# Thirty loads of 16-byte rows in SP's queue of a decode layer: one set before the ninth V, one before the last piece of the down weights

## The chip, the cores and the metric

The kernel runs on one core of one Trainium2 chip. The metric is the device time in microseconds (us); lower is better. Times of several runs are given as a median with the lowest and the highest.

## The reference, cut to what matters

One token of each of B = 4 sequences goes through attention over a cache and then through a gated MLP:

```python
q = (layernorm(x) @ wq)                       # 4 x 32 heads x 128
scores = einsum("bhqd,bhkd->bhqk", q, k_cache) * 128 ** -0.5   # 8192 keys
o = einsum("bhqk,bhkd->bhqd", softmax(scores), v_cache)
h = x + o @ wo                                # D = 512
g, u = layernorm(h) @ w_gate, layernorm(h) @ w_up              # F = 1792
out = h + (sigmoid(g) * u) @ w_down
```

The K cache and the V cache hold 4 x 32 x 8192 x 128 bf16 values each, 268.4 MB each. The weights together are 13.9 MB. All of it is read once.

## The kernel before, in words

The 128 pairs of sequence and head are worked off in NU = 32 units of four heads. A unit needs one K load and one V load of 8192 KB each; every load fills one of three slots of the buffer `KV` (128 partitions x 64 KB a slot). The list `order` gives the order of the loads: k0, k1, v0, k2, v1, ..., k31, v30, v31; entry n goes into slot n mod 3, so entry 18 is the ninth V (v8), which follows k9.

All large transfers are issued by SP, in this order (L466 to L500):

- `wq` (one load, L466), then the 63 whole K and V loads (L482). Entry n waits until entry n - 3 has been used up: a K until the DVE step `maxima` has passed the memset of `dummy` (L324), a V until the last matmul group of its weighted sum (L358). The last V, v31, is loaded in two halves `vh0`, `vh1` (L479).
- `wo` in three pieces of 2048, 1536 and 512 KB (L488), `wg` (L490) and `wu` in two pieces (L494), all of which wait for the last K to be used up.
- `wd` (the down weights) in three pieces `wd0`, `wd1`, `wd2` of 1024, 512 and 256 KB (`WDT`, L498), after v30 has been used up.
- half of the output (`out0`, L500); ACT issues `out1`. Then SP waits for both and ends (L502, L504).

Every DMA has a semaphore that counts 16 when it has landed (in `prog.dma`). SP works its list in order: what stands behind a waiting instruction waits too. Unit by unit, DVE transposes K in 16 chunks (`k_chunk`, L309), PE multiplies them with the query (L318), DVE finds the maxima (L324 to L331), ACT takes the exponential (L332), and PE forms the weighted sum of the V of the unit before (`pv`, L358, L374). At the end PE projects with `wo`, a layer norm follows, then gate and up (L432), and PE multiplies with `wd` in 14 steps (`down`, L457): steps 0 to 7 wait for `wd0`, 8 to 11 for `wd1`, 12 and 13 for `wd2`. DVE adds the residual (L463), and the two halves of the output go out.

Of the kernel before, what the change touches and what calls it, by code (L numbers as in the profile page):

```python
# [6 lines left out]
BF16 = mybir.dt.bfloat16  # L7
# [6 lines left out]
class _Prog:  # L14
# [51 lines left out]
    def emit(self, eng, fn, waits=(), incs=1, ch=None):  # L66
        todo = self._waits(eng, waits)
        key = ch or eng
        tok = self.token(key, incs) if incs else None
        self._put(eng, todo, key, fn, incs, 1)  # L70
        return tok
# [34 lines left out]
def bass_sequential_preLN__mha_block_cached__glu_gated_glu__decode_kernel(  # L106
# [13 lines left out]
    _, H, S, DH = A_k_cache.shape  # L120
# [15 lines left out]
    WDT = (0, 8, 12, 14)  # L136
# [3 lines left out]
    prog = _Prog({"p2d": "dve", "d2d": "dve", "a2d": "dve", "d2p": "pe", "a2p": "pe",  # L140
                  **{f"k{i}": "dve" for i in range(NSL)}, **{f"v{i}": "pe" for i in range(NSL)}})
    emit = prog.emit

    with ExitStack() as es:
        def SB(name, shape, dt):
            return es.enter_context(nc.sbuf_tensor(name, shape, dt))
# [19 lines left out]
        rs = SB("rs", [128, 1], FP32)  # L166
        ident = SB("ident", [128, 16], BF16)
        dummy = SB("dumm", [128, 2], FP32)

        kTb = kT[:, :].bitcast(BF16)  # L170
        KVw = KV[:, :].bitcast(FP32)
# [11 lines left out]
        def reg(slot, off, size):  # L183
            return KV[:, slot * SLOT + off:slot * SLOT + off + size]
# [20 lines left out]
        for k in keys:  # L205
# [12 lines left out]
        t_x = prog.dma("act", "x", lambda e: e.dma_start(x_bf, A_x.rearrange("b s d -> (b s) d")))  # L218

        t0 = emit("pool", lambda e: e.memset(ident[:, :], 0.0))  # L220
        t_ident = emit("pool", lambda e: e.affine_select(
            out=ident[:, :], in_=ident[:, :], compare_op=ALU.not_equal, fill=1.0, base=0,
            pattern=[[-1, 16]], channel_multiplier=1), [t0])
# [24 lines left out]
        def layernorm(src, waits, dst):  # L248
            a = emit("dve", lambda e: e.bn_stats(bst, src), waits)
            a = emit("dve", lambda e: e.bn_aggr(agg, bst), [a])  # L250
            a = emit("dve", lambda e: e.tensor_scalar(std[:, 0:1], agg[:, 1:2], EPS, None, op0=ALU.add), [a])
            a = emit("act", lambda e: e.activation(std[:, 1:2], std[:, 0:1], ACT.Sqrt), [a])
            a = emit("dve", lambda e: e.reciprocal(std[:, 0:1], std[:, 1:2]), [a])
            t_row = emit("dve", lambda e: e.tensor_scalar(
                row, src, agg[:, 0:1], std[:, 0:1], op0=ALU.subtract, op1=ALU.mult), [a])

            def f(e):
                ins = None
                for c in range(NC):
                    ins = e.matmul(cols(bank[XS], c), row[:, c:c + NC * 127 + 1:NC], ident[0:B, 0:B],  # L260
                                   start=(c == 0), stop=(c == NC - 1), skip_group_check=True)
                return ins
            a = emit("pe", f, [t_row, t_ident])
            return t_row, emit("dve", lambda e: e.tensor_copy(dst, bank[XS][:, 0:NC * B]), [a])
# [4 lines left out]
        _, t_xn = layernorm(x_bf, [t_x], xnT)  # L269
# [191 lines left out]
        for t in range(NFT):  # L461
# [4 lines left out]
        prog.dma("sp", "wq", lambda e: e.dma_start(reg(2, 0, NC * H * DH), A_wq.rearrange("(p c) f -> p (c f)", p=128)),  # L466
                 tok=t_wq)
        for n, (x, u) in enumerate(order):
            w = t_qp if n == 2 else None
            if n >= 3:  # L470
                y, o = order[n - 3]
                w = t_pv[o] if y == "v" else t_kd[o]
            slot = slots[x, u]
            halves = (x, u) == order[-1]
            cache = A_v_cache if x == "v" else A_k_cache
            src = cache[u % B, HU * (u // B):HU * (u // B + 1), :, :].rearrange("h (p r) d -> (h p) (r d)", p=32)
            if halves:
                for i in range(2):
                    prog.dma("sp", f"vh{i}", lambda e, src=src, slot=slot, i=i: e.dma_start(  # L479
                        reg(slot, i * SLOT // 2, SLOT // 2), src[:, i * SLOT // 2:(i + 1) * SLOT // 2]), [w], tok=t_vh[i])  # L480
                continue
            prog.dma("sp", f"{x}{slot}", lambda e, src=src, slot=slot: e.dma_start(reg(slot, 0, SLOT), src), [w],  # L482
                     tok=toks[x, u])
# [11 lines left out]
                reg(1, 16384 + (NC + 2 * i) * F, 2 * F), wu_src[:, 2 * i * F:2 * (i + 1) * F]), [k_done], tok=t_wu[i])  # L495
        wd_src = B_w_down.rearrange("(p t) f -> p t f", p=128)
        for i in range(len(WDT) - 1):
            prog.dma("sp", f"wd{i}", lambda e, i=i: e.dma_start(  # L498
                wd_v[:, WDT[i]:WDT[i + 1], :], wd_src[:, WDT[i]:WDT[i + 1], :]), [v_done], tok=t_wd[i])
        t_out = [prog.dma(("sp", "act")[x], f"out{x}", lambda e, x=x: e.dma_start(  # L500
            out.rearrange("b s d -> (b s) d")[:, HD * x:HD * (x + 1)], o_sb[32 * x:32 * x + B, :]), [t_o]) for x in range(2)]
        emit("sp", lambda e: e.nop(), t_out, incs=0)  # L502

        with nc.Block() as block:  # L504
            @block.sync
# [46 lines left out]
```

## Time and profile before

| | |
|---|---|
| time, median of 3 runs | 1283.34 us (1282.71 to 1283.39) |
| the profiled execution: time, span | 1282.72 us, 1281.0 us |
| bytes moved, mean rate over the span | 550.93 MB, 430 GB/s |
| PE, DVE, ACT busy | 784.0, 818.6, 51.1 us |
| SP's waits for DVE (L324) before a load | 1030.6 us in 31 waits |
| issue of k9, issue of v8 (SP) | 312.62 us, 346.90 us |
| issue of `wd0`, `wd1`, `wd2` (SP) | 1253.54, 1254.01, 1257.14 us |
| issue of the output (SP) | 1278.93 us |

Positions are us from the start of the span. A DMA issue on SP shows as an instruction of the queue (SPq); the transfer that it starts is seen in the DMA rows and in its time to landing. A transfer is cut into packets; the trace records the start, length and size of each packet, and the moment of each increment of a DMA's semaphore.

### The profile page before, as it was taken

To read this page: it belongs to the slowest core of one execution; us is meant where nothing else is said; L and a number is where in the kernel's file an instruction comes from. 1 tells how busy PE (TensorE), PEld (TensorE's weight loads), DVE (VectorE), ACT (ScalarE), POOL (GpSimd) and SP (SyncE) were. 2 spreads that over 40 slices of the span, in tenths; PEclk is the share of its full clock that TensorE was granted. 3 is DMA by queue.
4 is the path that set the end of the run, shared out by engine and by line. 5 is a ranking of instruction groups with operands and counts; after the bars stand their busy time and mean duration, and the time that the engine had idled before them with its cause. 6 is when DMAs were issued, how large, how long until landed. Compare 5 with 4: busy or idle time off the path is not lost. (4 is left out here: it accounts for less than half of the span.)

```text
span 1281.0 us, 13420 instructions
## 1 busy us (share of the span) xinstructions
PE 784.0 (61%) x5253; PEld 271.1 (21%) x5253; DVE 818.6 (64%) x1120; ACT 51.1 (4%) x106; POOL 4.3 (0%) x18
## 2 busy tenths in 40 slices
PE   1577665557755557655557655567555567555576
PEld 0122212122212222212222212222122222122222
DVE  2777776566665567665566765666766576756671
ACT  0000000000000000000000000000000000000001
POOL 1000000000000000000000000000000000000000
PEclk9998888789888799878898887898788898878897
DMA  9999999999999999999999999999999999999998
GB/s 426 424 425 430 449 426 426 434 445 430 426 436 440 434 426 436 438 436 426 432 436 442 426 428 434 446 428 426 436 444 430 426 436 440 434 426 436 436 424 330
DMA packets 11475, 550.93 MB, mean 430 GB/s; under 512 B 1212, under 2 KB 1224, under 8 KB 2760
## 3 DMA queue, kind: packets, MB, share of 16 engines
q1 hardware_dynamic: 11448, 550.77, 99.5%
q8 instruction: 7, 0.11, 0.0%
q14 instruction: 4, 0.03, 0.0%
q10 hardware_dynamic: 16, 0.01, 0.0%
HBM read 550.77 MB, written 0.00 MB: 430 GB/s over the span
## 5 line engine op out<-in xcount | busy, mean ns | idle before, releaser
L318 PE MATMUL PS<-kT,Lq 128*128 128x512 bf16 x2048 | 584.1, 416 | 442.7 <-PEq L51 428.6
L309 DVE STREAM_TRANSPOSE kT<-KV 128x1024 f32<-128x1024 f32 x512 | 617.5, 1233 | 199.5 <-DVEq L51 192.8
L318 PEld LDWEIGHTS PS<-kT,Lq 128*128 128x128 bf16 x2048 | 178.8, 103 | 849.3 <-issue 747.4
L358 PE MATMUL PS<-KV,PTz 128*16 128x512 bf16 x2048 | 120.5, 388 | 6.8 <-PEq L51 4.0
L381 DVE STREAM_TRANSPOSE kT<-PS 128x128 f32<-128x128 f32 x32 | 10.1, 317 | 144.6 <-DVEq L51 144.6
L338 DVE STREAM_TRANSPOSE PTz<-E_sb 32x512 bf16<-32x512 bf16 x128 | 89.9, 703 | 3.7 <-DVEq L51 0.7
L374 PE MATMUL PS<-kT,selc 128*1 128x128 f32 x1024 | 64.4, 403 | 28.2 <-PEq L51 27.9
L358 PEld LDWEIGHTS PS<-KV,PTz 128*16 128x16 bf16 x2048 | 58.7, 111 | 66.4 <-issue 20.7
L332 ACT ACTIVATE E_sb<-PS,negm 128x512 bf16<-128x512 f32 x32 | 22.0, 688 | 1171.6 <-DVE negm L331 1171.6
L325 DVE TENSOR_REDUCE mxp<-PS 128x1 f32<-128x512 f32 x32 | 22.1, 691 | 41.8 <-DVEq L51 41.8
L374 PEld LDWEIGHTS PS<-kT,selc 128*1 128x1 f32 x1024 | 27.6, 97 | 64.0 <-issue 43.6
L367 ACT ACTIVATE kT<-PS 128x512 f32<-128x512 f32 x32 | 19.1, 598 | 37.3 <-PE PS L358 37.3
L382 DVE TENSOR_SCALAR OT<-kT,rs 128x4 f32 (+1 forms) x32 | 7.3, 229 | 7.4 <-DVEq L51 7.2
L331 DVE STREAM_TRANSPOSE negm<-mxb 128x32 f32<-128x32 f32 x32 | 6.8, 212 | 4.7
L346 DVE STREAM_TRANSPOSE mxt<-mxb 128x32 f32<-128x32 f32 x32 | 6.8, 212 | 4.7
L302 DVE TENSOR_TENSOR Lq<-q_all,mask 128x32 bf16<-128x32 bf16 x32 | 9.8, 305 | 0.0
L327 DVE STREAM_TRANSPOSE mxt<-mxp 128x32 f32<-128x32 f32 x32 | 6.8, 212 | 4.7
L329 DVE TENSOR_SCALAR mxb<-mxr 128x32 f32<-128x32 f32 x32 | 5.8, 182 | 5.2 <-DVEq L51 0.6
L328 DVE TENSOR_REDUCE mxr<-mxt 128x1 f32<-128x32 f32 x32 | 6.0, 187 | 4.7
L344 DVE COPY mxb<-mxr 128x32 f32<-128x32 f32 x32 | 5.8, 181 | 4.7
L343 DVE TENSOR_REDUCE mxr<-mxt 128x1 f32<-128x16 f32 x32 | 5.4, 170 | 4.7
L347 DVE RECIPROCAL rs<-mxt 128x1 f32<-128x1 f32 x32 | 5.2, 164 | 4.7
(53 smaller groups left out, 60.9 us busy)
## 6 DMA issues: line engine op xcount, KB each, us to landing
KV<-in_A_v_cache_dram SPq DMA_DIRECT2D x2, 4096.0 KB, 46.2
KV<-in_A_wq_dram SPq DMA_DIRECT2D x1, 4096.0 KB, 12.2
KV<-in_A_wo_dram SPq DMA_DIRECT2D x1, 2048.0 KB, 23.1
KV<-in_B_w_gate_dram SPq DMA_DIRECT2D x1, 1792.0 KB, 29.4
KV<-in_B_w_up_dram SPq DMA_DIRECT2D x2, 896.0 KB, 22.0
KV<-in_A_wo_dram SPq DMA_DIRECT2D x1, 1536.0 KB, 26.5
KV<-in_B_w_down_dram SPq DMA_DIRECT2D x1, 1024.0 KB, 22.4
KV<-in_A_k_cache_dram SPq DMA_DIRECT2D x32, 50.5
```

What stands on the lines that cost most here:

```text
L302: t_lq[u] = emit("dve", lambda e, i: e.tensor_tensor(dst, bass.AP(raw(q_all), i * (4 * T3) + 4 * (u - T3 * t), [[NU * 4, 128], [1, 4], [0, ...
L309: t_tr[u, c] = emit("dve", lambda e: e.transpose(kT[:, (c % 2) * TW:(c % 2 + 1) * TW], KVw[:, o:o + TW]), w, ch="d2p")
L318: ins = e.matmul(bank[SBK], Lq[:, t, 31 - c:31 - c + 128], rhs, start=(c == 0 and t == 0), stop=(c == NT - 1 and t == 3))
L325: a = emit("dve", lambda e: e.tensor_reduce(mxp[:, 0:1], bank[SBK], AX.X, ALU.max), [t_sc[u, NT - 1], t_pool], ch="d2d")
L327: a = emit("dve", lambda e: e.transpose(mxt[:, :], mxp[:, :]), [a], ch="d2d")
L332: t_exp[u] = emit("act", lambda e: e.activation(E_sb[:, :], bank[SBK], ACT.Exp, bias=negm[:, 0:1], scale=SCALE, accum_out=sgp[:, 0:1]), [t ...
L338: return [e.transpose(PTz[32 * q:32 * (q + 1), :].rearrange("p (r q c) -> p r q c", r=4, q=4)[:, :, q, :], E_sb[32 * q:32 * (q + 1), :].re ...
L358: made.append(e.matmul(PS[32 * j:32 * j + 16, ob:ob + 512], lhsT, KV[:, slot * SLOT + 512 * k:slot * SLOT + 512 * (k + 1)], start=(k < 4), ...
L367: t_ocp[u] = emit("act", lambda e: e.activation(O_sb, bank[OBK], ACT.Copy), [t_pv[u]], ch="a2p")
L374: made.append(e.matmul(PS[32 * h:32 * h + 1, 512 * EX:512 * EX + 128], selc[:, 4 * h + q:4 * h + q + 1], rhs, start=(q == 0), stop=(q == 3 ...
L381: a = emit("dve", lambda e: e.transpose(OTf[:, :], bank[EX][:, 0:128]), [t_ex[u]], ch="d2d")
L382: t_ot[u] = emit("dve", lambda e, i: e.tensor_scalar(bass.AP(raw(OT), i * (4 * T3) + 4 * (u - T3 * t), [[NU * 4, 128], [1, 4]]), OTf[:, 0: ...
```

## The change

A tile `probe` (128 x 128 bf16) and thirty semaphores are added. `probes(n)` issues fifteen loads on SP: load m takes 8 values (16 bytes) from each of the first m rows of `wq` in HBM to the first m partitions of `probe`. One set is issued in front of entry 18 of the order (v8), the other in front of the last piece of the down weights (`wd2`). None of the thirty loads waits for anything, and nobody reads `probe`; SP's last instruction waits for all thirty semaphores besides the two of the output.

```diff
+        probe = SB("probe", [128, 128], BF16)
...
+        t_probe = {(n, m): None for n in range(2) for m in range(1, 16)}
+        for key in t_probe:
+            prog.sems["pr%d_%d" % key] = es.enter_context(nc.semaphore("s_pr%d_%d" % key))
+
+        def probes(n):
+            for m in range(1, 16):
+                t_probe[n, m] = prog.dma("sp", f"pr{n}_{m}", lambda e, m=m: e.dma_start(
+                    probe[0:m, 8 * m:8 * m + 8], A_wq[0:m, 0:8]))
...
         for n, (x, u) in enumerate(order):
+            if n == 18:
+                probes(0)
             w = t_qp if n == 2 else None
...
         for i in range(len(WDT) - 1):
+            if i == len(WDT) - 2:
+                probes(1)
             prog.dma("sp", f"wd{i}", lambda e, i=i: e.dma_start(
...
-        emit("sp", lambda e: e.nop(), t_out, incs=0)
+        emit("sp", lambda e: e.nop(), [*t_out, *t_probe.values()], incs=0)
```

In the compiled program SP has fifteen more waiting instructions at its end. They wait for the thirty probe semaphores, two at a time, and stand before the waits for the output, the last of them together with that for `out1`. The instructions of PE, DVE, ACT and GpSimd are the same, in the same order.

## The prediction

> **What bounds the kernel now.** I read the page's slices first, then its DMA queues, SP's waits, the chain that ended last, and SP's instructions at the end in order of time.
>
> ```profile
> PE   1577665557755557655557655567555567555576
> ...
> DMA  9999999999999999999999999999999999999998
> ...
> q1 hardware_dynamic: 11448, 550.77, 99.5%
> ```
>
> All 16 DMA engines work from the first slice to the last while PE is busy 5 to 7 tenths: the kernel lasts as long as its slowest DMA engine has packets, plus a short end. SP's waits show how much room its list has:
>
> ```profile
> SPq L482 <- DVE dumm L324: 1030.6, 31, 37.2
> SPq L482 <- PE PS L358: 130.1, 29, 4.5
> ```
>
> SP idles for most of the run, and a K load lands 50.5 us after its issue (page, DMA issues) though its bytes need 19.35 us (distance of two landings): more than one whole load is always queued behind the running one. At the end this turns:
>
> ```profile
> 1253.54 0.42 SPq L498
> 1253.96 0.05 issue
> 1254.01 23.15 DMA KV<-in_B_w_down_dram
> 1277.15 0.04 issue
> 1277.20 1.27 PE PS L457 x12
> ```
>
> The last steps wait for pieces of the down weights. The semaphore records say whose fault it is: fifteen increments of `wd2` arrive from 1274.65 to 1276.33, the sixteenth at 1277.79. One DMA engine runs 1.46 us behind the next and 3.14 us behind the first, and `wd1` shows the same (1275.73, then 1277.16). Delay on this engine moves the end one for one; delay on another is first taken up by 1.5 to 3.1 us of slack.
>
> **SP's time, first set.** It is issued when k9's issue has ended (312.95) and before v8's wait, which ends at 346.90, 33.9 us later. SP's issues cost 0.33 us on the 63 whole loads (0.57 at worst); the 4-row store takes 0.35. Fifteen at 0.35 are 5.3 us, at 0.57 8.6 us, both inside the wait: nothing. If the wait were gone, v8 would be issued 5.3 us later, and its 36.1 us to landing still cover that.
>
> **SP's time, second set.** Here SP is held back: the issue of `wg` takes 8.76 us, `wd1` 3.09, `wd2` 1.24. Counting packets issued less packets finished at the ends of the held issues (`wo2`, `wg`, `wd1`, `wd2`) gives 79, 80, 78 and 79 per engine: SP gets on when some packets have been finished. A set puts at most 30 packets on one engine (15 data, 15 increments). From 1257.1 the engines work on 4 KB packets of `wo` at 0.16 us, so 30 of them are 4.8 us; SP's own 15 x 0.35 = 5.3 us runs beside that. `wd2`, issued until 1258.38 now, would be issued until about 1263.7. Its first packet starts at 1273.43, and the first load of the run shows 1.0 us from issue (0.80) to first packet (1.83): 8.7 us to spare, cost nothing. `out0` stands behind it on SP and waits until 1278.93 anyway.
>
> **The DMA engines' time.** This is on the path. The 4-row store of `out0` shows how few rows are spread: its semaphore jumps at 1279.40, at the end of the issue, and then rises four times; its records hold four data packets and four increments. So m rows give m pairs of a 16-byte packet and an increment on m engines. The price of a pair: 4-byte increments take 9 ns and let the next packet start 6 ns later; at the other end the two output halves, whose 512-byte pairs follow each other on the same engines, start 29 to 45 ns apart. Packets of 2048 bytes cost 80 ns and of 4096 bytes 156 ns back to back, so a fixed part of 4 ns and the bytes. A pair of 16 bytes is therefore between 15 and 45 ns; I take 30, the middle, since the 16 bytes are nearer to the 4 and the engine must still fetch. An engine that is in every load carries 30 pairs: 0.9 us (0.45 to 1.35). Spread evenly, 240 pairs over 16 engines are 15 each: 0.45 us (0.23 to 0.68). The end moves by what falls on the slowest engine, and I do not know its place: if it is in all loads, +0.9; if in none, 0, since 1.35 us on any other engine stays below 1.46 us of slack. I take +0.45. The Trainium skill ("DMA: Bandwidth & Descriptors", "Why a DMA increments its semaphore by 16 and not by 1") says that such a DMA uses the lowest-numbered engines, as many as the rows; the four packets and the jump of the semaphore agree, which engines they are no view shows. By it one engine carries all 30 pairs, and the sum would be 0.9 or 0.
>
> **The waits at the end.** SP's issue of `out0` ends at 1279.29 and its wait for `out1` at 1280.20: 0.91 us idle. Fifteen waiting instructions at 17 ns each, with 0.04 us of issue between (chain), are 0.86 us and fit. At 0.1 us each they would be 1.5 us, 0.6 too long, but the wait for `out0` ends 0.41 us later still, so at most 0.2. I take 0. None can be held: the second set lies in the rings ahead of `wd2`, which has landed before.
>
> **Sum.** The profiled execution took 1282.72 us, its span and 1.72 around it; 0 + 0 + 0.45 + 0 makes 1283.2. It lies 0.62 below the median of 1283.34, so the forecast is 1283.8. About 0.2% (2.6 us) is what a measurement of this kernel can tell from no change; 0.45 is inside.
>
> **Rival 1, small writes that hold up their engine (slower).** The price above is that of sending. The records of landing say more: on the four engines of the output the second half's increments land 0.17 us after the first half's (1280.06 and 1280.24, 1280.18 and 1280.36), though they were sent 30 to 50 ns apart. Something takes 0.17 us per small DMA at the far end. If it holds the engine's stream back, 30 loads take 5.1 us on the engine that has them all; on the slowest engine this adds 5.1, on the first one 5.1 - 3.1 = 2.0 us, in the middle 3.5: 1286.8. The point from which it decides is 0.09 to 0.19 us a load: 2.6 us over 30 loads without slack, 5.7 with all of it. Against it: a large load's increment also waits for its data, and 8 packets of 2418 ns and one increment repeat every 19.35 us, so one increment costs 6 ns; fifteen in a row no row shows.
>
> The same with a longer price: each 16-byte write waits out a full trip. The shortest from an increment's packet to its landing is 0.30 us (load of `x`), so 30 are 9 us, less up to 3.1 of slack: 5.9 to 9.0, 1289 to 1292. The Trainium skill ("DMA: Bandwidth & Descriptors", "Specifications") states that writes under 512 bytes are done as read-modify-write; that speaks for this price if each trip is waited for. No data packet of under 512 bytes is in this trace's loads, so it stands neither confirmed nor refuted.
>
> **Rival 2, a queue of few places (slower).** If SP is held by the number of transfers in flight, not of packets, `wd2` comes late. At its issue eight are in flight now (`wo1` to `wd2`); with the probes 23. Were eight the limit, the eighth probe would wait for `wd1` (1277.16), and eight issues of 0.35 us take `wd2` to 1280.0; with 1.0 to its first packet, 0.64 for eight packets and 0.45 to land it is there at 1282.1 instead of 1277.79: +4.3, 1287.6. It decides as soon as a probe's issue takes over 1 us on average, 15.8 us from 1257.1 to 1272.9. For it: the issues here are slow; against it: `wd0` took 0.42 us with seven in flight.
>
> **Rival 3, the lag goes elsewhere (faster).** The slowest engine's lag grows in this trace from 2.50 to 3.48 us while a 16 KB instruction fetch runs (1242 us). SP's longer program can move a fetch to another engine. At best the end comes 1.46 us earlier: 1281.9, still within 0.2%; a larger gain needs the lag of seven engines to go, for which nothing speaks.
>
> **That the loads cost nothing at all** gives 1283.3 and belongs to the forecast.
>
> **Chances.** Forecast (no change within 0.2%, rival 3 in its likely size included): 0.56. Rival 1 at 0.17 us a load 0.21, at a full trip 0.10, rival 2 0.07: slower 0.38. Faster by over 0.2%: 0.06. The forecast alone spans 1281.9 to 1284.9 (1.46 less, or 1.35 and the waits' 0.2 more). The range takes in the first rival whole (1285.3 to 1288.5) and the second; its low end is cut to 1282.3. Left out are most of the full trip and half of the gains.
>
> **What the profile after would show.** In the packet records: 240 data packets of 16 bytes, 120 around 360 us (k9 lands about 363) and 120 between `wd1` and `wd2`. Right if SP's probe issues take about 0.35 us before the wait of L494 (formerly L482), `wd2` is issued by 1266, and the lag of the last engine at `wd2` stays between 1.5 and 4 us. Rival 1: one engine's packets behind the first set start 2.6 us or more late, and the lag at each later landing has grown by that. Rival 2: probe issues of over 1 us, and `wd2` landing as one late group of all engines. Wrong altogether if the rate before 1230 us is under 430 GB/s on all engines, or the final waits run past 1 us.

## The result and the profile after

The changed kernel takes 1285.69 us (18 runs, 1285.43 to 1285.96); the kernel before takes 1283.34 us in the same comparison. The ratio is 1.0019, with a 95% interval of 1.0012 to 1.0026: 2.35 us slower. That is inside the predicted range and, at 0.18%, just inside the 0.2% that the forecast allowed for no change, but five times the 0.45 us that its sum had. The profiled execution took 1285.75 us, its span is 1284.0 us.

The page's slices and its DMA queues, to be set beside those of before:

```profile
DMA  9999999999999999999999999999999999999997
...
q1 hardware_dynamic: 11928, 550.78, 99.4%
```

The 480 new packets are 240 of 16 bytes and 240 increments; the 16 engines still work from end to end. SP's waits:

```profile
SPq L494 <- DVE dumm L334: 1026.9, 31, 37.1
SPq L494 <- PE PS L368: 130.0, 29, 4.5
...
SPq L516 <- DMA out_dram<-KV: 0.2, 1, 0.2
```

SP's issues cost nothing: its waits for L334 before the loads are 3.7 us shorter in all (1030.6 before), less than the 5.28 us that the first set's issues take out of one of them. The last wait is shorter too (0.2 us, was 0.9), because fifteen added waits stand ahead of it. SP's instructions in order of time around the first set:

```profile
312.88 0.33 SPq L494 DMA_DIRECT2D KV<-in_A_k_cache_dram  x1
313.25 5.28 SPq L228 DMA_DIRECT2D probe<-in_A_wq_dram  x15
346.48 0.36 SPq L494 DMA_DIRECT2D KV<-in_A_v_cache_dram  x1
```

Its fifteen issues end 27.9 us before v8's. The rate while these packets pass is another matter. Two stretches, in each line the busy times and then granted clock, DMA share and GB/s, first before, then after:

```profile
340.00:360.00 20.00, 12.07 (x122) 4.60 (x120) 12.59 (x24) 1.38 (x3) 0.00 (x0) 0.98 1.00 433
360.00:365.00 5.00, 0.26 (x1) 0.14 (x2) 1.65 (x2) 0.00 (x0) 0.00 (x0) 0.50 1.00 433
```

```profile
340.00:360.00 20.00, 11.75 (x120) 4.57 (x120) 12.21 (x24) 1.37 (x3) 0.00 (x0) 0.94 1.01 433
360.00:365.00 5.00, 0.00 (x0) 0.00 (x1) 1.36 (x2) 0.00 (x0) 0.00 (x0) 0.50 0.97 354
```

For 5 us the DMA engines move 354 GB/s instead of 433: (433 - 354) x 5 us is 0.4 MB, 0.9 us of the whole rate. Packets of 64 KB make the rate of so short a stretch coarse, but the landings agree. Against two loads' distance (2 x 19.35 us) after v7's, v8's sixteen increments come 1.0 us late in the mean, the first 0.64 and the last 1.70 us, and the last engine keeps this to the end. Few bytes were added; the engines were held up, though the share counts them as busy.

The end of the chain that ended last:

```profile
1264.10 17.11 DMA KV<-in_B_w_down_dram
1281.20 0.04 issue
1281.25 0.43 PE PS L467 x4
```

Now the chain runs through `wd2`, and only the last four matmuls follow it; before, it ran through `wd1`, and twelve followed. The last piece lands 2.41 us after the piece ahead of it (1278.80 to 1281.20), before 0.63 us: +1.77 us. Not all of that counts. PE's instructions in order of time, after:

```profile
1277.69 1.75 PE L467 MATMUL PS<-KV 128*4 128x256 bf16 x24 [1.67 <-DMA KV<-in_B_w_down_dram]
1281.25 0.38 PE L467 MATMUL PS<-KV 128*4 128x256 bf16 x4 [1.80 <-DMA KV<-in_B_w_down_dram]
```

PE waits 1.80 us for the last piece. The granted clock was 1.00 in this stretch of this execution, so PE was through early with the first 24 matmuls. At a clock of 0.50 all 28 take 3.15 us when the last piece comes in time (e3, below); from the landing of the first piece, at 1277.56, they would end at about 1280.8 instead of 1281.7. Against such an execution about 0.8 us of the 1.77 remain.

### The profile page after: what moved, and what is told of

It is laid out like the page before. It is cut to its first block, busy times and chain, and to the rows that moved or that the text cites. A ratio compares the mean times of both kernels' runs of the same rounds, so it can differ in the third digit from the quotient of the medians.

```text
span 1284.0 us, 13465 instructions
## 1 busy us (share of the span) xinstructions
PE 785.2 (61%) x5253; PEld 271.3 (21%) x5253; DVE 818.2 (64%) x1120; ACT 51.0 (4%) x106; POOL 4.2 (0%) x18
## 5 line engine op out<-in xcount | busy, mean ns | idle before, releaser
L384 PE MATMUL PS<-kT,selc 128*1 128x128 f32 x1024 | 64.4, 403 | 28.1 <-PEq L51 27.9
```

The lines of the kernel that those rows point to most:

```text
L384: made.append(e.matmul(PS[32 * h:32 * h + 1, 512 * EX:512 * EX + 128], selc[:, 4 * h + q:4 * h + q + 1], rhs, start=(q == 0), stop=(q == 3 ...
```

## The experiments

Theory: each of the small loads costs an engine not its sending (12 ns) but the time of its increment, and the engine that lands last has 12 of the 15 loads of each set, those of 4 rows and more. In the trace after, on that engine, the increments of the second set land at 1278.98, 1279.16, 1279.35 and so on to 1281.02, every 0.17 to 0.20 us, and that of the last piece follows at 1281.20. Its 16-byte packets had been sent from 1278.31 to 1278.44, every 12 ns; then two packets of the last piece went, and the third took 0.90 us instead of 0.08. (The records name no engine; a packet is put to the engine whose packet before ends where it starts.) So the 1.77 us have three parts: 0.14 us of sending, 0.81 us of the one held packet, and 0.82 us because the last piece's own increment lands 1.29 us after it was sent, 0.46 before. Rivals: the 16-byte writes hold the engine; the 16-byte reads from HBM do; all engines meet at the same rows or partitions; SP's longer program.

Two measures stand beside each time. Step A is how much later v8's last increment lands than two loads' distance after v7's (0.00 us before). Step B is the distance from the last increment of `wd1` to that of `wd2` (0.63 us before). The median of the kernel before is 1283.2 to 1283.3 us in each comparison, and one comparison's ratio is known to about 0.09%.

**Each set alone.**

```diff
 # e1: without the second set
-            if i == len(WDT) - 2:
-                probes(1)
 # e2: without the first set
-            if n == 18:
-                probes(0)
```

> Only the first set (before v8). Theory (each small load's increment holds its DMA engine for 0.12 to 0.18 us, and the slowest engine, which has 12 of the 15 loads, moves the end): the lag that this engine gets at v8 in the trace after, 1.4 us, stays to the end: +0.9 to +1.4 us on the kernel before. Rival (the first set costs only its sending, and the rest of the loss is the end's): under +0.4 us. Rival (SP's longer program moves an instruction fetch, and that is the loss): about half of it, +1.2, with no step at v8.

> Only the second set (before the last piece of the down weights). Theory: the last increment of that piece lands 1.77 us later than by its distance from the piece before, and the end moves by +1.3 to +1.8 us; together with the first set alone about the +2.35 us of the whole change. Rival (the first set is all of it): under +0.4 us.

The first set alone: 1284.67 us, ratio 1.0011 (1.0002 to 1.0020), +1.40 us; step A 1.79, step B 0.64. The second alone: 1283.97 us, ratio 1.0006 (0.9997 to 1.0015), +0.70 us; its 11 runs (1283.88 to 1284.26) lie above all runs of before (up to 1283.59). Step A 0.02, step B 2.40. So 1.40 + 0.70 = 2.10 of the 2.35 us, and each set costs where its packets pass. The second was expected at 1.3 or more: its increment came as late as expected, the end did not. PE's instructions in order of time in e2, then in e3 (below), where the last piece is in time:

```profile
1275.82 2.72 PE L467 MATMUL PS<-KV 128*4 128x256 bf16 x24 [1.67 <-DMA KV<-in_B_w_down_dram]
1279.35 0.59 PE L467 MATMUL PS<-KV 128*4 128x256 bf16 x4 [0.81 <-DMA KV<-in_B_w_down_dram]
```

```profile
1275.97 3.15 PE L467 MATMUL PS<-KV 128*4 128x256 bf16 x28 [1.64 <-DMA KV<-in_B_w_down_dram]
```

At the clock of 0.50 that both have here, the steps take 3.15 us from the landing of the first piece if the others are in time. The last piece, 1.77 us late, holds PE up by 0.81 us only. The profiled execution of before had a clock of 0.75 there and took 2.36 us for the 28: 0.8 us less, which fits its 0.62 us under the median.

**Three rows or four.**

```diff
-            for m in range(1, 16):
+            for m in range(1, 9):
...
-                    probe[0:m, 8 * m:8 * m + 8], A_wq[0:m, 0:8]))
+                    probe[0:3, 8 * m:8 * m + 8], A_wq[0:3, 0:8]))   # e3; 0:4 in e4
```

> Each set is eight loads of 3 rows: three DMA engines get 8 pairs per set. In the trace after, the engine that lands last has the increments of the loads of 4 and more rows alone, so it is the fourth in order. Theory: it is not touched, and the three others have the slack for 2 x 8 x 0.15 = 2.4 us: within 0.3 us of the kernel before. Rival (SP, the number of loads, or any engine's delay counts): 16 of 30 loads, +1.2 us; the same as with 4 rows.

> Each set is eight loads of 4 rows, one row more than in the run with 3 rows. Theory: now the last engine gets 8 pairs per set instead of 12 in the whole change: 8/12 of 2.35 us, +1.6 us (1.2 to 2.1). Rival (number of loads or rows counts): the same as with 3 rows, within 0.3 us.

Three rows: 1283.05 us, ratio 0.9998 (0.9989 to 1.0007); step A 0.01, step B 0.63. Four rows: 1284.11 us, ratio 1.0006 (0.9997 to 1.0015), +0.84 us, with 11 runs from 1283.78; step A 0.65, step B 1.67. The fourth row makes the whole difference: the end belongs to one engine, the fourth that a load of few rows takes, and 16 loads on three other engines vanish in their slack. Step B shows 1.04 us for 8 loads (0.13 each) where the whole change has 1.77 for 12 (0.15 each). The landings explain both: the increments of the set and then that of the last piece land 0.185 us apart in the mean, 9 x 0.185 = 1.67 us here and 13 x 0.185 = 2.41 us in the whole change, and 0.63 us of that passed before as well. Step A is 0.65 for 8 (0.08 each) and 1.70 for 12 (0.14 each): the price in the first set is not even, and why stays open. The time was expected at +1.2 to +2.1; the cover by PE took the rest, as in e2.

**One increment for twelve writes.**

```diff
-            for m in range(1, 16):
-                t_probe[n, m] = prog.dma("sp", f"pr{n}_{m}", lambda e, m=m: e.dma_start(
-                    probe[0:m, 8 * m:8 * m + 8], A_wq[0:m, 0:8]))
+            t_probe[n, 1] = prog.dma("sp", f"pr{n}_1", lambda e: e.dma_start(
+                probe[0:16, 0:120].rearrange("p (m c) -> p m c", c=10)[:, :, 0:8],
+                A_wq[0:16, 0:120].rearrange("p (m c) -> p m c", c=10)[:, :, 0:8]))
```

> Each set is one load of 12 rows of 16 bytes to each of 16 partitions: every DMA engine gets 12 data packets of 16 bytes per set, as many as the last engine has in the whole change, but one increment instead of 12. Theory (the increments hold the engine): 2 x (12 x 12 ns + 0.18) = +0.3 to +0.6 us. Rival (each 16-byte write holds the engine, as a read-modify-write would): as the whole change, +2.3 us or more.

1284.78 us, ratio 1.0012 (1.0003 to 1.0021), +1.48 us: the theory, as it stood, fell. Step B is 0.60, so in the second set twelve 16-byte packets with one increment cost nothing to be seen, as the theory says. But step A is 2.28 us, more than in the whole change. In the first set something else than the increments can cost as much. (The executions scatter from 1283.83 to 1284.98 us, and the profiled one is among the fastest, at 1283.88.)

**The second set with longer rows, and behind the last piece; the first set spread out.**

```diff
 # e6: second set alone, rows of 512 bytes
+                    reg(2, 16384 + 256 * m, 256)[0:m, :], A_wq[0:m, 0:256]))
 # e7: second set alone, behind the loop over the down weights
+        probes(1)
         t_out = [prog.dma(("sp", "act")[x], ...
 # e8: first set alone, load n - 17 in front of entry n
+            if 18 <= n < 33:
+                probes(0, n - 17)
```

> Only the second set, with rows of 512 bytes instead of 16 (into a free part of the slot of the down weights). Theory: the increments take their time whatever the rows are; the data packets of about 23 ns lie inside it: the same as the second set alone within 0.4 us, +1.3 to +1.9 us. Rival (writes under 512 bytes are what costs): 12 x 35 ns = +0.4 us.

> Only the second set, issued behind the last piece of the down weights instead of before it. Theory: its increments come after those that PE waits for and are used up while PE and DVE work; the output's increments are 2 us later: 0 to +0.3 us. Rival (the loads cost wherever they stand in the queue): as the second set alone.

> Only the first set, its fifteen loads one by one in front of fifteen successive K and V loads. Theory: one increment more per 19 us has landed long before the next; what is left is the sending, 12 x 12 ns, 0 to +0.4 us. Rival (each load costs its engine 0.12 us wherever it stands): as the first set alone, +0.9 to +1.4 us.

Rows of 512 bytes: 1284.26 us, ratio 1.0010 (1.0001 to 1.0019), +0.96 us, step B 2.40, as with 16 bytes to 0.01 us: the size of the rows does not matter, the number of loads does. The time was expected at +1.3 us or more; as in e2, the increment came as late as expected and the end did not. Behind the last piece: 1283.12 us, ratio 1.0000 (0.9991 to 1.0009); step B 0.65. The same fifteen loads are free where the pieces that PE waits for stand ahead of them. Spread out: 1283.24 us, ratio 1.0000 (0.9991 to 1.0009), step A 0.02. One more small load per 19 us is free as well; it is the burst that costs.

**What the first set's price is.** Three runs with the first set alone change where its rows come from and go to.

```diff
-                    probe[0:m, 8 * m:8 * m + 8], A_wq[0:m, 0:8]))
 # e9: from SBUF (the first load waits for t_ident, long done)
+                    probe[0:m, 8 * m:8 * m + 8], ident[0:m, 0:8]), [t_ident] if m == 1 else [])
 # e10: from 120 different rows of HBM
+                    probe[0:m, 8 * m:8 * m + 8], B_w_gate[32 * m:32 * m + m, 0:8]))
 # e11: to 120 different partitions
+                    probe[m * (m - 1) // 2:m * (m + 1) // 2, 0:8], A_wq[0:m, 0:8]))
```

> Only the first set, its rows read from the tile ident in SBUF instead of from HBM. The first set alone cost +1.4 us, and one load of 12 runs with a single increment cost as much at v8, so the increments are not its whole price. Theory A (small reads from HBM that hold up the engine between the long ones): under +0.5 us. Theory B (small writes or pairs as such, whatever their source): as the first set alone, +1.2 to +1.6 us.

> Only the first set, its 120 rows read from 120 different rows of the gate weights instead of from the same fifteen rows of wq. Theory A1 (the same few rows of HBM are asked by all engines at once): under +0.7 us. Theory A2 (any small read from HBM waits behind the long ones) and theory B (small writes or pairs as such): as the first set alone, +1.2 to +1.6 us.

> Only the first set, its 120 rows written to 120 different partitions instead of to the first fifteen. Theory B1 (all engines write the same few partitions at once, and their ports hold them up): under +0.7 us. Theory A and theory B2 (each small write holds its own engine): as the first set alone, +1.2 to +1.6 us.

From SBUF: 1284.58 us, ratio 1.0011 (1.0001 to 1.0020), step A 1.68. From spread rows: 1284.47 us, 1.0009 (1.0000 to 1.0018), step A 1.48. To spread partitions: 1284.60 us, 1.0011 (1.0001 to 1.0020), step A 1.63. All three as the first set alone: no crowding at rows of HBM or at partitions, and without any read from HBM the price is there. In e9 the packets of a set again go out every 12 ns (thirteen on the last engine, as the one-row load takes eight engines here), and the next packet of 64 KB takes up to 4.34 us instead of 2.42: this is the second set's picture, increments that land slowly and an engine that is held. Then e5's price, with one increment, must be another, and the last run puts the question to both at once:

```diff
-                A_wq[0:16, 0:120].rearrange("p (m c) -> p m c", c=10)[:, :, 0:8]))
+                bass.AP(raw(ident), 0, [[16, 16], [0, 12], [1, 8]])), [t_ident])
```

> Each set is one load of 12 rows of 16 bytes to each of 16 partitions, as in the run with one load of 12 runs (+1.5 us, with +2.3 us on the last engine at v8), but read from SBUF. Theory (two prices that hide each other: an increment takes 0.14 us of its engine, and 16-byte reads from HBM behind 64 KB reads hold it up for as long): neither is left, +0.3 us or less, no step at v8 over 0.3 us. Rival (small writes hold the engine, read-modify-write): the step of 2.3 us at v8 stays, +1.4 us or more.

1283.44 us, ratio 1.0002 (0.9993 to 1.0011), +0.24 us; step A 0.29, step B 0.61. With few increments and no small reads from HBM hardly more than the sending is left. The 192 writes of a set are those of e5, of 16 bytes in the same places: read from HBM they make step A 2.28 us, read from SBUF 0.29 us. The stretch in which they pass, e5 and then e12; the last column is GB/s:

```profile
358.00:368.00 10.00, 2.91 (x7) 1.00 (x8) 3.99 (x7) 0.00 (x0) 0.00 (x0) 0.50 0.89 354
```

```profile
358.00:368.00 10.00, 3.19 (x8) 1.01 (x8) 4.27 (x7) 0.00 (x0) 0.00 (x0) 0.52 1.03 433
```

In e5 the 16-byte packets of the engines that come last are spread from 362.59 to 364.95 us, and 64 KB packets begun between 359.6 and 360.6 us take 2.99 to 3.42 us. In e12 an engine sends its twelve within 0.07 us, and such 64 KB packets take 2.44 to 2.59.

So there are two prices. A run of small loads costs its engine about 0.14 us for each load, whatever the rows are (e6, e9). Whether this is the increment's own time or each increment's wait for the write ahead of it, no run here separates. A run of 16-byte reads from HBM among 64 KB reads costs as much or more (e5), and among packets of 4 and 2 KB none (its step B). In the change both act at the same place in the first set and do not add up: 1.79 us with both (e1), 1.68 with the increments alone (e9). The last engine's packets show how: in e9 its pairs go out in 0.16 us and its next 64 KB packet takes 4.00 us; in e1 the pairs need 0.94 us and the next 64 KB packet takes 2.86. In both the increments land 0.18 to 0.19 us apart, so the slow reads pass in time that the landings need anyway. Why small reads cost among long ones stays open.

## Why the prediction was right or wrong

**What bounds.** Right: the last DMA engine sets the end. e3 and e4 show it as no view of before could: one row more, +1.06 us.

**SP's time.** Right in both places. The first set takes 5.28 us inside the wait (5.3 predicted). The second takes 5.31 us, and `wd2` is issued until 1264.80, when its packets are still over 9 us away on the first engine; 1263.7 was predicted, and all of the end is 1.7 us later. This ends rival 2: with 23 transfers in flight no small load's issue takes over 0.38 us in this trace. (In e2, e4 and e7 the longest issue of a set takes 1.1 to 1.3 us, but the mean stays under 0.5; the rival needed over 1 us on average.)

**The waits at the end.** Right: SP still waits 0.2 us for `out1` when the fifteen waits are through.

**The price of a pair.** This is the step that failed: the prediction put the price of sending for the whole price. It took 30 ns, between the 15 of two increments and the 45 of two output halves. Sending is cheaper than that, 12 ns a pair, but on the engine that counts a load costs 0.14 to 0.15 us (1.70 and 1.77 us for 12 loads), because the increments land only every 0.185 us and hold up what is behind them. The bound of 45 ns came from two pairs in a row, and two are let through: the engine that lands last sent twelve pairs 12 ns apart and two packets of 2 KB before it was held. Rival 1 had read the right number for a burst, 0.17 us between the landings of two halves of the output, and asked the right question, whether the stream behind is held back. It is. The 2.6 us that this rival named as its sign behind the first set did not come, 1.70 did: 12 of the 15 loads reach the last engine.

**Where the pairs fall.** The last engine gets 12 loads of a set, neither none nor all: the loads of 1, 2 and 3 rows leave it out. The prediction's two ends, all or none, bracket it. The rule that it cited from the Trainium skill ("DMA: Bandwidth & Descriptors", "Why a DMA increments its semaphore by 16 and not by 1") is that such a load takes as many engines as it has rows, the lowest-numbered. It fits as far as the runs show: loads of 3 rows leave the last engine alone (e3) and loads of 4 rows do not (e4). Which number the engine has no run shows. But "0.9 or 0" did not follow: loads of 1 to 15 rows that each take the first engines give the first 15 loads, the fourth 12 and the fifteenth one.

**The sum.** 24 loads at 0.14 to 0.15 us are 3.5 us on the last engine, and 2.35 arrive. The second set's 1.77 us lie beside PE's last matmuls for all but about 0.8, which leaves 2.5 us, 0.15 more than measured. This is the second term that the prediction had wrong, though it did no harm there: it let `wd2`'s delay move the end one for one. But steps 0 to 11 take 2.72 us at a clock of 0.50 (e2), longer than the 1.86 us by which the last piece followed the first before. That the change stayed within the forecast's 0.2% is luck. The price was five times too small, and 2.35 us stay under 2.6 only because three loads of a set miss the last engine and PE covers some 0.9 us of the second set; without either it would be 3.2 to 3.3 us, an estimate from these prices.

**The other rivals.** The full trip per small write is not what the runs show: in e12 twelve writes of 16 bytes on each engine cost 0.3 us or less, and in a run of loads the increments land 0.185 us apart, not 0.30. The Trainium skill ("DMA: Bandwidth & Descriptors", "Specifications") states read-modify-write for writes under 512 bytes. That it is waited for write by write, e12 speaks against; that it makes the price of a load, e6 does, whose rows of 512 bytes cost the same. Rival 3, that the instruction fetches move: in the trace after, the last engine's lag grows by 0.9 us around the fetch at 1244 us, in the trace of before by 1.0 (2.43 to 3.44 us by the landings, where the prediction has 2.50 to 3.48); no gain and no loss.

**The signs.** The prediction allowed the last engine a lag of 1.5 to 4 us at `wd2` if it was right. The lag is 5.9 us (3.1 before), so this sign spoke against the forecast although the time lies in its range.

## What to carry to other kernels

Count small transfers by their number on the engine that finishes last, not by their bytes: in a burst here their increments landed 0.185 us apart, which cost that engine some 0.15 us for each load, and everything queued behind waited. Small reads from HBM between long ones had a price of their own. Spread over other traffic, put behind what is waited for, or kept to fewer rows than reach that engine, the same loads were free. Where one engine finishes late, its packets are the critical path, and a cost on the others shows only beyond their slack.

## What the runs showed of the hardware

- An engine lets 12 small pairs go out in 0.14 us, but their increments land one by one, 0.17 to 0.20 us apart, and the increment of the transfer behind them lands only after them, 0.18 us behind the last. Meanwhile one data packet is held: a 2 KB packet took 0.90 us instead of 0.08 (after), a 64 KB packet up to 4.34 instead of 2.42 (e9).
- One increment between large loads costs 6 ns (before). The price of an increment in a burst cannot be read from it.
- Twelve 16-byte reads from HBM on each engine, among 64 KB reads, delayed the last engine by 2.28 us (e5); from SBUF by 0.29 us (e12).
- The one-row load of eight values went out as one packet of 16 bytes when it came from HBM, and as eight packets of 2 bytes on eight engines when it came from `ident` in SBUF (e9).
